# Cached grouped-query attention: K loaded one transfer further ahead, P*V two steps behind, a transposed last P*V, and three V loads with one head group in two half copies

## The chip, the cores and the metric

The kernel runs on one core of one Trainium2 chip. Its engines are TensorE (PE), VectorE (DVE), ScalarE (ACT), GpSimd (POOL) and SyncE (SP), each with a queue of its own, and 16 DMA engines move data between HBM and SBUF. The metric is the device time of one execution in microseconds, as the median of the runs.

## The reference

```python
B, Sq, D = 32, 4, 1024
Hq, Hkv, Sk, Dh = 32, 4, 2048, 128            # everything in bf16

q = (x @ wq).reshape(B, Sq, Hq, Dh).transpose(0, 2, 1, 3)
k = repeat(k_cache, 8, axis=1); v = repeat(v_cache, 8, axis=1)   # caches: [B, 4, 2048, 128]
p = softmax(einsum("bhqd,bhkd->bhqk", q, k) * Dh ** -0.5)
o = einsum("bhqk,bhkd->bhqd", p, v)
return o.transpose(0, 2, 1, 3).reshape(B, Sq, Hq * Dh) @ wo
```

Each of the 32 batch entries has 4 queries of 32 heads. Eight heads share one of the 4 head groups of the caches. The caches are 2 MB of K and 2 MB of V per batch entry, and each byte is used once.

## The kernel before

The loop runs over the batch entries, one per step i. The 4 queries x 8 heads of one head group make 32 rows, and the 4 groups make the 128 rows of the score tile.

Loads. `load_k(b)` (line 132) brings the K of entry b in one transfer of 2048 KB into one of three buffers; it waits until PE has transposed the K that was there (`("fill", b - 3, 7)`). `load_v(b)` (line 137) brings V in the same way into one of three buffers and waits for the P*V that last used it (`("pv", b - 3)`). For the last entry V comes in four transfers, one for each head group. All loads are issued by SP in one queue, in program order; SP stops at the first wait that isn't met. The order is x, four parts of wq, K0, K1, and then for each b: K(b+2), V(b), and for b = 2 to 5 a quarter of wo (lines 152 to 159).

A step i of the loop (lines 320 to 343), in the order in which the engines get it:

1. `pe_qk(i)` (line 235): 16 matmuls give the scores in PSUM (`ps_s`). `softmax_max(i)`: DVE takes the row maximum and scales it.
2. `pe_ot(i-2)`, `ot_evac(i-2)`: the output of entry i-2 is transposed into `oT_sb`. After every eighth entry `oproj` multiplies 32 tokens with wo.
3. `pe_fill(i+1, f)` and `evac(i+1, f)` (lines 201 to 219), f = 0 to 7: PE transposes the next K tile in eight parts, and DVE and ACT copy the parts to `KT_sb`. `softmax_exp(i)` stands after the first two parts on ACT and writes P, not normalised, to `P_sb`; `softmax_rinv(i)` gives one over the row sums.
4. `pe_pv(i-1)` (line 254): 64 matmuls, 16 for each head group, with P^T stationary; `o_evac(i-1)` scales by one over the sum.
5. `pe_pt(i, f)`, `evac_pt(i, f)` (lines 221 to 232): PE transposes P, and DVE copies it to `PT_sb`, once P*V of entry i-1 is done with that buffer.

So P*V runs one step behind its scores, and V(b) follows K(b+2) in the queue. PE's small outputs go through a ring of four PSUM banks (`slot`, line 194), in program order.

After the loop (lines 346 to 378) the last entry is finished by itself: P*V of three head groups, then of the fourth; each result is scaled by ACT, transposed by PE, copied by DVE, and then used by the output projection of the last 32 tokens: 24 heads, then 8. The result is copied to `y_sb`, and the stores go out on SP and ACT.

All waits are semaphore counts, written down by the small planner `_Program` (line 13): each operation names what it waits for, and each engine runs its list in order.

Of the kernel before, what the change touches and what calls it, by code (L numbers as in the profile page):

```python
# [5 lines left out]
ACT = mybir.ActivationFunctionType  # L6
ALU = mybir.AluOpType
AX = mybir.AxisListType
BF16 = mybir.dt.bfloat16
F32 = mybir.dt.float32  # L10


class _Program:
# [43 lines left out]
def bass_standalone__gqa_block_cached__sampling_kernel(  # L57
# [8 lines left out]
    B, Sq, D = x.shape  # L66
    _, G, Sk, Dh = k_cache.shape
# [8 lines left out]
    TV = T // C  # L76
    KT = D // 128
    NKB = 3
    NVB = 3
    NFILL = 8  # L80
    TB = T // NFILL
    NRING = 4
    OG = 8
    NOG = B // OG
    NC = D // 4
    scale = float(Dh) ** -0.5
# [5 lines left out]
    with ExitStack() as es:  # L92
        def sbuf(name, shape, dtype):
            return es.enter_context(nc.sbuf_tensor(name, shape, dtype))
# [4 lines left out]
        V_sb = sbuf("V_sb", [128, NVB, G, TV, Dh], BF16)  # L99
        KT_sb = sbuf("KT_sb", [128, TV, G, R * C], BF16)  # L100
        QT_sb = sbuf("QT_sb", [128, B, Hq, Sq], BF16)
        oT_sb = sbuf("oT_sb", [128, Hq, NT], BF16)
        P_sb = sbuf("P_sb", [128, Sk], BF16)
        PT_sb = sbuf("PT_sb", [128, TV, 128], BF16)
        x_sb = P_sb[:, 0:D]
        xT_sb = P_sb[:, D:2 * D].rearrange("p (a b) -> p a b", b=128)
        o_sb = sbuf("o_sb", [128, Dh], BF16)
# [15 lines left out]
        p = _Program()  # L123
# [8 lines left out]
        def load_k(b):  # L132
            p.dma("sp", lambda e: e.dma_start(
                K_sb[:, b % NKB, :, :], k_cache[b].rearrange("g (r t) d -> (g r) t d", r=R)),
                [("fill", b - NKB, NFILL - 1)] if b >= NKB else [], ("k", b), f"s_k{b % NKB}")

        def load_v(b):
            src = v_cache[b].rearrange("g (p t) d -> p g (t d)", p=128)
            dst = V_sb[:, b % NVB, :, :, :].rearrange("p g t d -> p g (t d)")
            waits = [("pv", b - NVB)] if b >= NVB else []  # L140
            if b < B - 1:
                p.dma("sp", lambda e: e.dma_start(dst, src), waits, ("v", b), f"s_v{b % NVB}")
            else:
                for g in range(G):
                    p.dma("sp", lambda e, g=g: e.dma_start(dst[:, g, :], src[:, g, :]), waits, ("v", b, g), f"s_vl{g}")
# [3 lines left out]
                wo_sb[:, 8 * c:8 * c + 8, :], wo[c * 1024:(c + 1) * 1024, :].rearrange("(h p) n -> p h n", p=128)),  # L149
                ["qproj"], ("wo", c), f"s_w{c}")  # L150

        load_k(0)
        load_k(1)
        for b in range(B):
            if b + 2 < B:
                load_k(b + 2)
            load_v(b)
            if b in (2, 3, 4, 5):
                load_wo(b - 2)
# [34 lines left out]
        def slot(free):  # L194
            n = len(freed)
            freed.append(free)
            return ring[n % NRING], [freed[n - NRING]]
# [13 lines left out]
        def evac(b, f):  # L211
            buf = slot_of["kt", b, f]
            waits = [("fill", b, f)] + ([("qk", b - 1)] if b else [])
            dst = KT_sb[:, f * TB // C:(f + 1) * TB // C, :, :].rearrange("p v g (r c) -> p (v g) r c", c=C)
            src = buf.rearrange("p (c m r) -> p m r c", c=C, r=R)
            if f in DVE_FILLS:
                p.op("dve", lambda e: e.tensor_copy(dst, src), waits, ("kt", b, f))  # L217
            else:
                p.op("act", lambda e: e.activation(dst, src, ACT.Copy), waits, ("kt", b, f))  # L219

        def pe_pt(i, f):
            buf, waits = slot(("pt", i, f))
            buf = slot_of["pt", i, f] = buf.bitcast(BF16)
            for q in range(8):
                p.op("pe", lambda e, q=q: e.transpose(  # L225
                    buf[:, q * 128:(q + 1) * 128], P_sb[:, (8 * f + q) * 128:(8 * f + q + 1) * 128], ident[:, :]),
                    waits + [("exp", i)] if q == 0 else [], ("ptf", i, f) if q == 7 else None)

        def evac_pt(i, f):
            buf = slot_of["pt", i, f]  # L230
            p.op("dve", lambda e: e.tensor_copy(PT_sb[:, 8 * f:8 * f + 8, :].rearrange("p t q -> p (t q)"), buf),  # L231
                 [("ptf", i, f)] + ([("pv", i - 1)] if i else []), ("pt", i, f))


        def pe_qk(i):
# [11 lines left out]
        def pv_mm(buf, i, g, t, waits, done):  # L247
            p.op("pe", lambda e: e.matmul(  # L248
                buf[32 * g:32 * (g + 1), 0:Dh],
                lhsT=PT_sb[:, t, 32 * g:32 * (g + 1)],  # L250
                rhs=V_sb[:, i % NVB, g, t, :],
                start=(t == 0), stop=(t == TV - 1), tile_position=(0, 32 * g)), waits, done)

        def pe_pv(i):
            buf, waits = slot(("o", i))
            slot_of["o", i] = buf
            waits = waits + [("pt", i, 0), ("pt", i, 1), ("v", i)]
            for t in range(TV):
                for g in range(G):
                    pv_mm(buf, i, g, t, waits if t == 0 and g == 0 else [],  # L260
                          ("pv", i) if (t, g) == (TV - 1, G - 1) else None)

        def o_evac(i):
            buf = slot_of["o", i]
            p.op("act", lambda e: e.activation(o_sb[:, :], buf[:, 0:Dh], ACT.Copy, scale=rinv[:, i:i + 1]),  # L265
                 [("pv", i), ("rinv", i)] + ([("oT", i - 1)] if i else []), ("o", i))

        def pe_ot(i):
            buf, waits = slot(("ot", i))
            buf = slot_of["ot", i] = buf.bitcast(BF16)  # L270
            p.op("pe", lambda e: e.transpose(buf[:, 0:128], o_sb[:, :], ident[:, :]), waits + [("o", i)], ("oT", i))  # L271

        def ot_evac(i):
            buf = slot_of["ot", i]
            p.op("act", lambda e: e.activation(  # L275
                oT_sb[:, :, i * Sq:(i + 1) * Sq], buf[:, 0:128].rearrange("p (h s) -> p h s", s=Sq), ACT.Copy),
                [("oT", i)], ("ot", i))
# [38 lines left out]

        for f in range(NFILL):
            pe_fill(0, f)
            evac(0, f)
        for i in range(B):  # L320
            pe_qk(i)
            softmax_max(i)
            if i >= 2:
                pe_ot(i - 2)
                ot_evac(i - 2)
                if i % OG == 1 and i > 1:
                    oproj(i // OG - 1)
            if i + 1 < B:
                for f in (0, 1):
                    pe_fill(i + 1, f)  # L330
                    evac(i + 1, f)
            softmax_exp(i)
            if i + 1 < B:
                for f in range(2, NFILL):
                    pe_fill(i + 1, f)
                    evac(i + 1, f)
            softmax_rinv(i)
            if i >= 1:
                pe_pv(i - 1)
                o_evac(i - 1)  # L340
            for f in range(2):
                pe_pt(i, f)
                evac_pt(i, f)


        L = B - 1
        pe_ot(L - 1)
        ot_evac(L - 1)
        o_l, waits = slot(None)
        waits = waits + [("pt", L, 0), ("pt", L, 1)]  # L350
        for t in range(TV):
            for g in range(3):
                pv_mm(o_l, L, g, t, waits + [("v", L, k) for k in range(3)] if t == 0 and g == 0 else [],
                      ("pva", L) if (t, g) == (TV - 1, 2) else None)
        for t in range(TV):
            pv_mm(o_l, L, 3, t, [("v", L, 3)] if t == 0 else [], ("pv", L) if t == TV - 1 else None)
        p.op("act", lambda e: e.activation(o_sb[0:96, :], o_l[0:96, 0:Dh], ACT.Copy, scale=rinv[0:96, L:L + 1]),
             [("pva", L), ("rinv", L), ("oT", L - 1)], "oa")
        p.op("act", lambda e: e.activation(o_sb[96:128, :], o_l[96:128, 0:Dh], ACT.Copy, scale=rinv[96:128, L:L + 1]),
             [("pv", L)], "ob")  # L360
        ta, waits = slot(None)
        ta = ta.bitcast(BF16)
        p.op("pe", lambda e: e.transpose(ta[:, 0:96], o_sb[0:96, :], ident[0:96, 0:96]), waits + ["oa"], "oTa")
        p.op("dve", lambda e: e.tensor_copy(
            oT_sb[:, 0:24, L * Sq:(L + 1) * Sq], ta[:, 0:96].rearrange("p (h s) -> p h s", s=Sq)), ["oTa"], "ota")
        y_l = ps_s[:, 0:512]
        n = NOG - 1
        oproj_mm(y_l, n, range(24), ["ota", ("ot", L - 1)], None)
        tb, waits = slot(None)
        tb = tb.bitcast(BF16)  # L370
        p.op("pe", lambda e: e.transpose(tb[:, 0:32], o_sb[96:128, :], ident[96:128, 96:128]), waits + ["ob"], "oTb")
        p.op("dve", lambda e: e.tensor_copy(
            oT_sb[:, 24:32, L * Sq:(L + 1) * Sq], tb[:, 0:32].rearrange("p (h s) -> p h s", s=Sq)), ["oTb"], "otb")
        oproj_mm(y_l, n, range(24, 32), ["otb"], ("op", n))
        oproj_evac(y_l, n)
        for m in range(NOG - 1):
            oproj_out(m, ("sp",))
# [57 lines left out]
```

## Time and profile before

| | |
|---|---|
| median of 9 runs | 387.18 us (385.95 to 387.56) |
| profiled execution, its own time | 386.93 us |
| its span, first to last instruction | 385.1 us |
| PE busy | 279.0 us (72%) |
| DVE busy | 273.8 us (71%) |
| ACT busy | 208.6 us (54%) |
| DMA queue of the loads (q1) | 151.49 MB, 96.2% of 16 engines' span |
| K loads | 32 x 2048 KB, 24.9 us from issue to landing |
| V loads | 31 x 2048 KB, 27.0 us; 4 x 512 KB, 15.7 us |

Busy time counts an engine's own instructions, and DMA time is counted in engine time of 16 DMA engines. The time from issue to landing of a load includes its time in the queue behind earlier loads. The mean granted TensorE clock is 0.954 of full speed. A chain of work follows the execution back from its last instruction, from each step to what released it.

### The profile page before, as it was taken

What the parts mean: (1) busy time and instruction counts of PE and PEld (TensorE: products, weight loads), DVE (VectorE), ACT (ScalarE), POOL (GpSimd) and SP (SyncE); (2) the same over time, 40 slices, a digit from 0 to 9 for tenths busy, and PEclk for the clock granted to TensorE, in tenths of its full rate; (3) what the DMA queues carried; (4) which work ended last, traced back from release to release, by engine and by line L of the source; (5) the groups of instructions that cost most, each with busy time, mean ns of one, the idle gap of its engine ahead of it and who ended that gap; (6) DMA issues with size and microseconds to landing.
All of it is one profiled execution on the core that took longest, in us unless ns stands there. A gap on an engine that the chain in (4) does not pass through costs nothing.

```text
span 385.1 us, 12595 instructions
## 1 busy us (share of the span) xinstructions
PE 279.0 (72%) x5929; PEld 227.2 (59%) x5929; DVE 273.8 (71%) x299; ACT 208.6 (54%) x261; POOL 0.7 (0%) x6
## 2 busy tenths in 40 slices
PE   2876888655383967888777778877758878876756
PEld 1875766535272856666655566665647666665545
DVE  0016999783552984899888849998868858997850
ACT  1005777455161646676666627766646557666620
POOL 0000000000000000000000000000000000000000
PEclk9998999996977899999999999999998999999978
DMA  8999999999999999999999999999999999999930
GB/s 327 434 425 419 416 419 397 413 412 395 411 403 416 417 419 413 418 413 419 416 416 421 415 416 416 416 411 418 415 418 419 418 415 421 413 421 411 380 149 9
DMA packets 27251, 152.32 MB, mean 395 GB/s; under 512 B 1472, under 2 KB 1984, under 8 KB 22592
## 3 DMA queue, kind: packets, MB, share of 16 engines
q1 hardware_dynamic: 27104, 151.49, 96.2%
q8 instruction: 46, 0.75, 0.8%
q10 hardware_dynamic: 96, 0.03, 0.0%
q14 instruction: 5, 0.04, 0.0%
HBM read 151.26 MB, written 0.26 MB: 393 GB/s over the span
## 4 chain that ended last, share of the span: by engine, by line
DMA 58%; PE 17%; ACT 12%; DVE 10%; issue 2%; SPq 0%
DMA K_sb<-in_k_cache_dram 52%; ACT KT_sb L219 6%; DMA w_sb<-in_wq_dram 6%; ACT P_sb L285 6%; DVE KT_sb L217 5%; DVE mx L280 4%; PE ps_r L207 3%; PE ps_r L248 3%; PE ps_r L296 3%; PE ps_s L240 3%; PE ps_r L225 3%; PE ps_s L296 1%; PE ps_s L176 1%; DVE QT_sb L187 0%; DVE PT_sb L231 0%
## 5 line engine op out<-in xcount | busy, mean ns | idle before, releaser
L207 PE MATMUL ps_r<-ident,K_sb 128*128 128x128 bf16 x2048 | 140.7, 227 | 66.6 <-DMA K_sb<-in_k_cache_dram 39.3
L217 DVE COPY KT_sb<-ps_r 128x1024 bf16<-128x1024 bf16 x128 | 147.9, 1215 | 38.8 <-PE ps_r L207 38.7
L207 PEld LDWEIGHTS ps_r<-ident,K_sb 128*128 128x128 bf16 x2048 | 123.5, 102 | 82.9 <-DMA K_sb<-in_k_cache_dram 41.5
L219 ACT ACTIVATE KT_sb<-ps_r 128x1024 bf16<-128x1024 bf16 x128 | 124.5, 1026 | 72.1 <-PE ps_r L207 71.9
L280 DVE TENSOR_REDUCE mx<-ps_s 128x1 f32<-128x2048 f32 x32 | 73.3, 2291 | 7.6 <-PE ps_s L240 7.3
L285 ACT ACTIVATE P_sb<-ps_s,negmx 128x2048 bf16<-128x2048 f32 x32 | 63.0, 1970 | 2.1 <-DVE negmx L281 2.1
L231 DVE COPY PT_sb<-ps_r 128x1024 bf16<-128x1024 bf16 x64 | 41.4, 686 | 16.6 <-PE ps_r L225 15.0
L248 PE MATMUL ps_r<-V_sb,PT_sb 128*32 128x128 bf16 x2048 | 36.7, 222 | 17.1 <-ACT KT_sb L219 12.3
L248 PEld LDWEIGHTS ps_r<-V_sb,PT_sb 128*32 128x32 bf16 x2048 | 31.0, 98 | 22.7 <-ACT KT_sb L219 19.4
L275 ACT ACTIVATE oT_sb<-ps_r 128x128 bf16<-128x128 bf16 x31 | 8.6, 278 | 55.6 <-PE ps_r L271 55.6
L225 PE MATMUL ps_r<-ident,P_sb 128*128 128x128 bf16 x512 | 35.1, 223 | 2.0 <-ACT P_sb L285 1.4
L240 PE MATMUL ps_s<-KT_sb,QT_sb 128*32 128x512 bf16 x512 | 34.7, 389 | 2.3 <-DVE KT_sb L217 1.7
L225 PEld LDWEIGHTS ps_r<-ident,P_sb 128*128 128x128 bf16 x512 | 29.4, 99 | 5.6 <-ACT P_sb L285 1.6
L240 PEld LDWEIGHTS ps_s<-KT_sb,QT_sb 128*32 128x32 bf16 x512 | 10.9, 96 | 13.3 <-issue 3.3
L187 DVE CAST QT_sb<-ps_r 128x512 bf16<-128x512 f32 x2 | 1.3, 686 | 22.4 <-PE ps_r L176 22.4
L265 ACT ACTIVATE o_sb<-ps_r,rinv 128x128 bf16<-128x128 f32 x31 | 11.4, 367 | 9.6 <-PE ps_r L248 9.6
L189 ACT ACTIVATE QT_sb<-ps_r 128x512 bf16<-128x512 f32 x2 | 1.1, 594 | 25.9 <-PE ps_r L176 25.9
L176 PE MATMUL ps_s<-P_sb,w_sb 128*128 128x128 bf16 x128 | 9.3, 230 | 7.4 <-DMA w_sb<-in_wq_dram 7.4
L296 PE MATMUL ps_r<-w_sb,oT_sb 128*32 128x256 bf16 x384 | 11.5, 273 | 3.5 <-issue 2.3
L176 PEld LDWEIGHTS ps_s<-P_sb,w_sb 128*128 128x128 bf16 x128 | 8.1, 103 | 8.0 <-issue 4.3
L296 PEld LDWEIGHTS ps_r<-w_sb,oT_sb 128*32 128x32 bf16 x384 | 10.0, 97 | 4.6 <-issue 3.4
L271 PEld LDWEIGHTS ps_r<-ident,o_sb 128*128 128x128 bf16 x31 | 3.0, 98 | 12.7 <-issue 12.7
(30 smaller groups left out, 58.7 us busy)
## 6 DMA issues: line engine op xcount, KB each, us to landing
K_sb<-in_k_cache_dram SPq DMA_DIRECT2D x32, 2048.0 KB, 24.9
V_sb<-in_v_cache_dram SPq DMA_DIRECT2D x31, 2048.0 KB, 27.0
w_sb<-in_wq_dram SPq DMA_DIRECT2D x4, 2048.0 KB, 14.8
w_sb<-in_wo_dram SPq DMA_DIRECT2D x4, 2048.0 KB, 24.6
V_sb<-in_v_cache_dram SPq DMA_DIRECT2D x4, 512.0 KB, 15.7
P_sb<-in_x_dram SPq DMA_DIRECT2D x1, 256.0 KB, 2.8
out_dram<-y_sb SPq DMA_DIRECT2D x14, 16.0 KB, 11.6
out_dram<-y_sb ACTq DMA_DIRECT2D x2, 16.0 KB, 1.6
```

Source lines behind the costliest of these rows:

```text
L176: p.op("pe", lambda e, kt=kt, h=h: e.matmul(ps_q(h), lhsT=w_sb[:, kt, h * Dh:(h + 1) * Dh], rhs=xT_sb[:, kt, :], start=(kt == 0 and h % 4 ...
L207: p.op("pe", lambda e, q=q, t=t: e.transpose(buf[:, q * 128:(q + 1) * 128], K_sb[:, b % NKB, t, :], ident[:, :]), waits + [("k", b), "iden ...
L217: p.op("dve", lambda e: e.tensor_copy(dst, src), waits, ("kt", b, f))
L219: p.op("act", lambda e: e.activation(dst, src, ACT.Copy), waits, ("kt", b, f))
L225: p.op("pe", lambda e, q=q: e.transpose(buf[:, q * 128:(q + 1) * 128], P_sb[:, (8 * f + q) * 128:(8 * f + q + 1) * 128], ident[:, :]), wai ...
L231: p.op("dve", lambda e: e.tensor_copy(PT_sb[:, 8 * f:8 * f + 8, :].rearrange("p t q -> p (t q)"), buf), [("ptf", i, f)] + ([("pv", i - 1)] ...
L240: p.op("pe", lambda e, c=c, g=g: e.matmul(ps_s[32 * g:32 * (g + 1), c * 512:(c + 1) * 512], lhsT=QT_sb[:, i, REP * g:REP * (g + 1), :], rh ...
L248: p.op("pe", lambda e: e.matmul(buf[32 * g:32 * (g + 1), 0:Dh], lhsT=PT_sb[:, t, 32 * g:32 * (g + 1)], rhs=V_sb[:, i % NVB, g, t, :], star ...
L265: p.op("act", lambda e: e.activation(o_sb[:, :], buf[:, 0:Dh], ACT.Copy, scale=rinv[:, i:i + 1]), [("pv", i), ("rinv", i)] + ([("oT", i - ...
L280: p.op("dve", lambda e: e.tensor_reduce(mx[:, i:i + 1], ps_s[:, :], AX.X, ALU.max), [("qk", i)], ("mx", i))
L285: p.op("act", lambda e: e.activation(P_sb[:, :], ps_s[:, :], ACT.Exp, bias=negmx[:, i:i + 1], scale=scale, accum_out=ssum[:, i:i + 1]), [( ...
L296: p.op("pe", lambda e, h=h, j=j: e.matmul(buf[32 * j:32 * (j + 1), 0:NC], lhsT=oT_sb[:, h, 32 * n:32 * (n + 1)], rhs=wo_sb[:, h, NC * j:NC ...
```

## The change

Four things change.

- The loads: K0, K1 and K2 are issued first, and then K(b+3) before V(b). So each K goes out one transfer earlier in the queue than before.
- P*V of an entry runs two steps behind its scores (`pe_pv(i - 2)`), and its output is transposed three steps behind. For that `PT_sb` has two buffers, and the copy of P^T waits for the P*V of two entries before.
- The last entry: P is multiplied by one over its sums on DVE before it is transposed. Its P*V then has V as the stationary operand, so that it gives the transposed output o^T of one head group straight away; four such groups alternate with the four parts of the last output projection. The scaling on ACT and the transposes of the output are gone for this entry.
- V of entries 7, 15 and 23: head groups 0 to 2 come in one transfer, and group 3 in two copies for 64 partitions each. The DRAM side of these copies has 8 rows as its outer dimension.

```diff
+def _load_low_half(nc, eng, dst, src):
+    assert src.shape[0] == 8 and eng.engine == mybir.EngineType.SP
+    return eng.add_instruction(mybir.InstDMACopy(
+        name=nc.get_next_instruction_name(),
+        engine=eng.engine,
+        mode="Copy",
+        queue="qSPDynamicHW",
+        cce_op=ALU.bypass,
+        ins=[eng.lower_ap_dma(src)[0]],
+        outs=[eng.lower_ap_dma(dst)[0]],
+    ))
...
+    LOW_V = (7, 15, 23)
...
-        PT_sb = sbuf("PT_sb", [128, TV, 128], BF16)
+        PT_sb = sbuf("PT_sb", [128, 2, TV, 128], BF16)
...
-            if b < B - 1:
+            if b in LOW_V:
+                p.dma("sp", lambda e: e.dma_start(dst[:, 0:3, :], src[:, 0:3, :]), waits, ("v", b, 0), f"s_v{b % NVB}")
+                low = v_cache[b, 3].rearrange("(j a t) d -> j a (t d)", j=2, a=8)
+                for j in range(2):
+                    p.dma("sp", lambda e, j=j: _load_low_half(nc, e, dst[64 * j:64 * (j + 1), 3, :], low[j]),
+                          waits, ("v", b, 1) if j == 0 else ("v", b), "s_vlow")
+            elif b < B - 1:
...
-        load_k(0)
-        load_k(1)
+        for b in range(NKB):
+            load_k(b)
         for b in range(B):
-            if b + 2 < B:
-                load_k(b + 2)
+            if b + NKB < B:
+                load_k(b + NKB)
             load_v(b)
...
-                 [("ptf", i, f)] + ([("pv", i - 1)] if i else []), ("pt", i, f))
+                 [("ptf", i, f)] + ([("pv", i - 2)] if i > 1 else []), ("pt", i, f))
...
-            if i >= 2:
-                pe_ot(i - 2)
-                ot_evac(i - 2)
-                if i % OG == 1 and i > 1:
+            if i >= 3:
+                pe_ot(i - 3)
+                ot_evac(i - 3)
+                if i > OG and i % OG == 2:
                     oproj(i // OG - 1)
...
-            if i >= 1:
-                pe_pv(i - 1)
-                o_evac(i - 1)
+            if i >= 2:
+                pe_pv(i - 2)
+                o_evac(i - 2)
+            if i == L:
+                p.op("dve", lambda e: e.tensor_scalar(P_sb[:, :], P_sb[:, :], rinv[:, L:L + 1], None, op0=ALU.mult),
+                     [("rinv", L)], ("pn", L))
             for f in range(2):
-                pe_pt(i, f)
+                pe_pt(i, f, ("pn", L) if i == L else ("exp", i))
                 evac_pt(i, f)
...
+        pe_ot(L - 2)
+        ot_evac(L - 2)
+        pe_pv(L - 1)
+        o_evac(L - 1)
...
+        def pv_last(g):
+            buf, waits = slot(None)
+            for t in range(TV):
+                p.op("pe", lambda e, t=t: e.matmul(
+                    buf[:, 0:32], lhsT=V_sb[:, L % NVB, g, t, :], rhs=PT_sb[:, L % 2, t, 32 * g:32 * (g + 1)],
+                    start=(t == 0), stop=(t == TV - 1)),
+                    waits + [("v", L, g), ("pt", L, 0), ("pt", L, 1)] if t == 0 else [],
+                    ("pvl", g) if t == TV - 1 else None)
+            p.op("dve", lambda e: e.tensor_copy(
+                oT_sb[:, 8 * g:8 * (g + 1), L * Sq:(L + 1) * Sq], buf[:, 0:32].rearrange("p (h s) -> p h s", s=Sq)),
+                [("pvl", g)], ("otl", g))
+
+        def oproj_last(g):
+            oproj_mm(y_l, n, range(8 * g, 8 * (g + 1)), [("otl", g), ("ot", L - 1), ("exp", L)],
+                     ("op", n) if g == G - 1 else None)
+
+        pe_ot(L - 1)
+        ot_evac(L - 1)
+        pv_last(0)
+        for g in range(G):
+            if g + 1 < G:
+                pv_last(g + 1)
+            oproj_last(g)
```

The old code for the last entry (lines 349 to 374 of the kernel before) is taken out.

More of the change, by code (lines that the diff above doesn't have):

```diff
@@ L219, in evac, with pe_pt @@
                 p.op("act", lambda e: e.activation(dst, src, ACT.Copy), waits, ("kt", b, f))
-        def pe_pt(i, f):
+        def pe_pt(i, f, ready):
             buf, waits = slot(("pt", i, f))
@@ L226, in pe_pt @@
                     buf[:, q * 128:(q + 1) * 128], P_sb[:, (8 * f + q) * 128:(8 * f + q + 1) * 128], ident[:, :]),
-                    waits + [("exp", i)] if q == 0 else [], ("ptf", i, f) if q == 7 else None)
+                    waits + [ready] if q == 0 else [], ("ptf", i, f) if q == 7 else None)
         def evac_pt(i, f):
             buf = slot_of["pt", i, f]
-            p.op("dve", lambda e: e.tensor_copy(PT_sb[:, 8 * f:8 * f + 8, :].rearrange("p t q -> p (t q)"), buf),
-                 [("ptf", i, f)] + ([("pv", i - 1)] if i else []), ("pt", i, f))
+            p.op("dve", lambda e: e.tensor_copy(PT_sb[:, i % 2, 8 * f:8 * f + 8, :].rearrange("p t q -> p (t q)"), buf),
+                 [("ptf", i, f)] + ([("pv", i - 2)] if i > 1 else []), ("pt", i, f))
         def pe_qk(i):
@@ L249, in pv_mm @@
                 buf[32 * g:32 * (g + 1), 0:Dh],
-                lhsT=PT_sb[:, t, 32 * g:32 * (g + 1)],
+                lhsT=PT_sb[:, i % 2, t, 32 * g:32 * (g + 1)],
                 rhs=V_sb[:, i % NVB, g, t, :],
@@ L256, in pe_pv @@
             slot_of["o", i] = buf
-            waits = waits + [("pt", i, 0), ("pt", i, 1), ("v", i)]
+            waits = waits + [("pt", i, 0), ("pt", i, 1), ("v", i)] + ([("v", i, 0)] if i in LOW_V else [])
             for t in range(TV):
@@ L319, in bass_standalone__gqa_block_cached__sampling_kernel @@
             evac(0, f)
+        L = B - 1
         for i in range(B):
@@ L322, in bass_standalone__gqa_block_cached__sampling_kernel @@
             softmax_max(i)
-            if i >= 2:
-                pe_ot(i - 2)
-                ot_evac(i - 2)
-                if i % OG == 1 and i > 1:
+            if i >= 3:
+                pe_ot(i - 3)
+                ot_evac(i - 3)
+                if i > OG and i % OG == 2:
                     oproj(i // OG - 1)
-            if i + 1 < B:
+            if i < L:
                 for f in (0, 1):
@@ L332, in bass_standalone__gqa_block_cached__sampling_kernel @@
             softmax_exp(i)
-            if i + 1 < B:
+            if i < L:
                 for f in range(2, NFILL):
@@ L343, in bass_standalone__gqa_block_cached__sampling_kernel @@
                 evac_pt(i, f)
-        L = B - 1
+        pe_ot(L - 2)
+        ot_evac(L - 2)
+        pe_pv(L - 1)
+        o_evac(L - 1)
+        y_l = ps_s[:, 0:512]
+        n = NOG - 1
+        def pv_last(g):
[9 more added lines that the diff above has]
+                [("pvl", g)], ("otl", g))
@@ L347, in bass_standalone__gqa_block_cached__sampling_kernel @@
+        def oproj_last(g):
+            oproj_mm(y_l, n, range(8 * g, 8 * (g + 1)), [("otl", g), ("ot", L - 1), ("exp", L)],
+                     ("op", n) if g == G - 1 else None)
         pe_ot(L - 1)
         ot_evac(L - 1)
[L349 to L371, printed above, removed]
@@ L372, in bass_standalone__gqa_block_cached__sampling_kernel @@
-        p.op("dve", lambda e: e.tensor_copy(
-            oT_sb[:, 24:32, L * Sq:(L + 1) * Sq], tb[:, 0:32].rearrange("p (h s) -> p h s", s=Sq)), ["oTb"], "otb")
-        oproj_mm(y_l, n, range(24, 32), ["otb"], ("op", n))
+        pv_last(0)
[3 more added lines that the diff above has]
+            oproj_last(g)
         oproj_evac(y_l, n)
```

## The prediction

> **What bounds the kernel now.** I read the slices of the page, then the DMA queues, then the last 36 us in stretches, then the chain of work that ended last. From the page:
>
> ```profile
> PEclk9998999996977899999999999999998999999978
> DMA  8999999999999999999999999999999999999930
> GB/s 327 434 425 419 416 419 397 413 412 395 411 403 416 417 419 413 418 413 419 416 416 421 415 416 416 416 411 418 415 418 419 418 415 421 413 421 411 380 149 9
> q1 hardware_dynamic: 27104, 151.49, 96.2%
> q8 instruction: 46, 0.75, 0.8%
> HBM read 151.26 MB, written 0.26 MB: 393 GB/s over the span
> ```
>
> The DMA engines are full from the second slice to the 37th, near 416 GB/s. PE is busy for 72%, DVE for 71%; neither is the bound. A 2048 KB load (2.097 MB) costs 2.097 / 416 = 5.04 us. The bytes stay, so only what happens after the last bytes, or how these end, can be gained. Now the end in stretches; the last two columns are DMA share and GB/s:
>
> ```profile
> core 0: us, PE busy (x) PEld busy (x) DVE busy (x) ACT busy (x) POOL busy (x), PEclk, DMA share, GB/s
> 362.00:364.00 2.00, 0.82 (x15) 0.49 (x16) 2.00 (x3) 2.00 (x4) 0.00 (x0) 1.00 1.03 404
> 364.00:366.00 2.00, 2.00 (x84) 1.79 (x88) 1.06 (x3) 1.18 (x2) 0.00 (x0) 1.00 0.74 280
> 366.00:368.00 2.00, 1.17 (x18) 0.39 (x17) 1.85 (x3) 0.28 (x1) 0.00 (x0) 1.00 0.58 224
> 368.00:370.00 2.00, 1.02 (x61) 0.88 (x64) 1.51 (x2) 0.42 (x1) 0.00 (x0) 1.00 0.50 199
> 370.00:372.00 2.00, 0.58 (x15) 0.41 (x16) 0.16 (x1) 1.89 (x3) 0.00 (x0) 0.60 0.50 191
> 372.00:374.00 2.00, 1.69 (x16) 1.42 (x14) 1.07 (x2) 0.28 (x1) 0.00 (x0) 0.50 0.29 92
> ```
>
> Half of the 16 engines run dry near 365; the other half works alone, at half the rate, until 373.7 (the last V load is issued at 357.96 and lands 15.7 us later). The shares from 364 on add up to (0.74 + 0.58 + 0.50 + 0.50 + 0.29) x 2 = 5.2 us of all 16 engines: dealt out evenly, the loads would end near 369.3. One group of 8 is some 8 us behind the other. Then the chain, start and length in us:
>
> ```profile
> 333.92 24.47 DMA K_sb<-in_k_cache_dram
> 358.44 0.63 PE ps_r L207 x8
> ...
> 369.58 2.07 ACT P_sb L285 x2
> 371.64 0.05 issue
> 371.69 1.90 PE ps_r L225 x16
> ...
> 374.36 3.08 PE ps_r L248 x61
> ...
> 377.89 2.81 PE ps_s L296 x96
> ```
>
> The end hangs on the last K tile, which lands on its slowest engine at 358.40. From there to the end of the span is 26.7 us: transposing K, scores, softmax, P^T, P*V, output projection. V lands just before P^T is ready, so it does not decide. PEclk is 0.50 in this stretch: 64 P*V matmuls take 3.08 us, where they take 1.08 us at full clock (358 to 366).
>
> [...]46 packets of 0.75 MB in all on q8. They take 0.8% x 16 x 385 = 49 us of engine time; dealt to 8 engines that is 6.2 us each, near the 8 us lag. That is my reading of the lag, not shown. [...]PEclk is 0.5 from 370.4 to 377.2[...].
>
> **The change, part by part.**
>
> *K one transfer earlier.* The order of the tail goes from K30 V28 K31 V29 V30 V31 to K31 V28 V29 V30 V31. K31 lands one load earlier: -5.04 us. The price is less cover elsewhere. At the start V0 no longer lies between K2 and K3. K3 waits for the transposes of K0 and is issued at 34.2; K2 (issued at 4.03, 35.3 us to landing) ends at 39.3 on the slowest engine and a little before 38 on the others, so K3 still queues some 2 us before the rings run dry: nothing, at worst 1 to 2 us. Later, V(b) waits for a P*V two steps behind: its issue comes about 10 - 5 = 5 us later against its slot. Around V28 to V30 a load waits 25 to 28 us from issue to landing, some 20 us of that in the queue, so 5 us less is hidden. V31 was the tightest, 15.7 us to landing, and stays behind V29 and V30 in the queue, 10 us of transfers.
>
> *P^T in two buffers, P*V a step later.* Same instructions, same order within a step; the copy of P^T then waits for the P*V of two steps ago, issued just ahead of it, as now. Nothing. But for the last two steps it moves work: P*V of step 30 now stands behind the last P^T instead of ahead of it.
>
> *Three loads with low halves.* Per load, 512 KB goes to 8 engines instead of 16. Each of the 8 gets 32 KB more, the other 8 get 32 KB less; 32 KB at 26 GB/s (416 / 16) is 1.26 us. Three loads: 3.8 us either way, which is half of the 8 us lag. If the low half is the early one, K31 and V31 land 3.8 us earlier on the late engines, and the two halves end together near 369.9 (373.7 - 3.8). SP gets 6 more DMA issues of about 1.2 us (L145's own are 0.3 to 1.3), in a queue that waits 10 us a step: nothing.
>
> *The tail.* K31 lands at 358.40 - 5.04 - 3.8 = 349.6. Up to the end of the last exp the work is the same and takes 371.64 - 358.40 = 13.2 us, since V28 and V29 land within it (354.6, 359.7): 362.8. Then
> - reciprocal and its wait 0.2: 363.0.
> - new: P times 1/sum, 128x2048 in bf16. The trace has no such row[...]. 363.7.
> - P^T 1.9 at half clock[...]: 365.7. The transpose of step 29, 0.2: 365.9.
> - P*V of step 30, 3.1 at half clock; V30 landed at 364.7. 369.0. Its copy and its transpose, with waits, 0.7: 369.7.
> - removed: the old last P*V, two copies, two transposes and their copies.
> - new: 4 groups of 16 matmuls with V stationary, 128 columns, and 32 moving. The nearest rows are the transposes (L176, 16 in 0.89 us at full clock: 56 ns); the moving side is a quarter. [...]I take 45: 0.7 a group, 2.8 in all.
> - output projection 4 x 32 matmuls at 29 ns (L296, 96 in 2.81): 3.7. The copies on DVE (about 0.2) lie under the next group. V31 lands at 369.9 and its last group is wanted near 373.5: not on the path.
> - 376.2; pipeline end, copy of y 0.7; then the last stores, which took 385.1 - 382.6 = 2.5: 379.4.
>
> The span falls from 385.1 to 379.4. The profiled execution's own time was 386.93, 1.8 over its span, and the median of the runs is 0.25 above that: 379.4 + 1.8 + 0.25 = 381.4. In sum: -5.0 (K slot), -3.8 (balance), +3.1 (a longer tail: 29.8 us from K31 instead of 26.7).
>
> **The rivals.**
> 1. *The low half is the late half.* The trace does not number the engines. Then K31 lands 3.8 later instead of earlier, at 357.2, and the sum gives 381.4 + 7.6 = 389.0: slower. It decides once the shift makes the late engines more than 2 us later. For it: nothing but that half and half are alike in the page. Against it: the size, 3.8 us on each side, is just half of the lag.
> 2. *The copies run on all engines, or the lag is not tied to fixed engines.* Only the slot and the tail are left: 381.4 + 3.8 = 385.2, a small gain.
> 3. *PE bounds the end.* The final matmuls find PE still at half clock, where a transpose took 119 ns (1.90 / 16) instead of 56[...]: 384.5 to 386.3.
> 4. The other way: PE stays at full clock after the idle stretch. Then P^T and P*V take 1.0 and 1.1 and the end is 2.9 earlier, 378.5.
>
> **How the numbers follow.** The forecast with rival 4 as its good end: 0.70, its own range 378.4 to 384.5. Rival 1: 0.12. Rival 2: 0.08. Rival 3: 0.10. The predicted time is 381.4. The range leaves out rival 1 and the better edge: 378.4 to 386.6. About 0.2% (0.8 us) can be told from no change. Faster: 0.70, nearly all of rival 2 and most of rival 3, 0.84. Same: 0.04. Slower: 0.12, rival 1.
>
> **What would show it.** In the changed kernel's profile the DMA share should stay near 1.0 until 367 or later and drop to zero within 3 us, with no stretch at 0.5; if the stretch at 0.5 grows to some 15 us, rival 1 is right; if it keeps its 8 us, rival 2. The last K tile should land near 349.6 and the last exp end near 362.8. The matmuls of the new last P*V should take about 0.7 us a group; over 1.2 us, with PEclk at 0.5, is rival 3. A share under 0.9 between 35 and 60 us would mean that the shorter cover at the start cost time.

## The result

The changed kernel takes 397.92 us (median of 10 runs, 395.46 to 399.14) against 387.18 us before. The ratio is 1.027, with a 95% interval of 1.026 to 1.029: 10.7 us slower. The prediction was 381.4 us and faster. Its profiled execution took 398.35 us, with a span of 396.6 us against 385.1.

From the page of the changed kernel, the slices of the span and the queue of the loads:

```profile
DMA  8999999999999999999999999999999999999860
GB/s 342 421 426 420 416 418 397 407 401 411 410 396 413 416 258 417 418 416 415 418 414 416 333 334 414 417 418 414 418 415 418 321 357 415 401 415 403 328 249 26
...
q1 hardware_dynamic: 26816, 151.49, 96.6%
```

The bytes are the same as before, and the DMA engines are as busy. But three times they are busy and move much less: 258 GB/s near 144 us, 333 and 334 near 228 us, 321 and 357 near 317 us (the middle of the slices). These are the places of entries 7, 15 and 23, the three loads with half copies. Against 416 GB/s the five slices of 9.9 us lack 158 + 83 + 82 + 95 + 59 = 477 GB/s, or 4.7 MB: 11.4 us at the full rate. That alone is larger than the slowdown.

The packets of the changed kernel by size:

```profile
DMA packets 26963, 152.32 MB, mean 384 GB/s; under 512 B 1520, under 2 KB 2032, under 8 KB 22256
```

and of the kernel before:

```profile
DMA packets 27251, 152.32 MB, mean 395 GB/s; under 512 B 1472, under 2 KB 1984, under 8 KB 22592
```

The 92 DMAs of before leave 16 packets under 512 B each (92 x 16 = 1472), one for each engine by my reading. The six half copies add 48, 8 each: they run on 8 engines. The prediction had assumed this, and its "low half" is these 8 engines; the trace does not number them.

The first of the three closer up, in stretches of the changed kernel (the last two columns are DMA share and GB/s):

```profile
134.00:138.00 4.00, 3.17 (x99) 2.19 (x92) 3.72 (x6) 1.36 (x3) 0.00 (x0) 1.00 1.09 429
138.00:142.00 4.00, 3.51 (x59) 3.17 (x59) 3.95 (x5) 3.44 (x3) 0.00 (x0) 1.00 1.00 224
142.00:146.00 4.00, 0.49 (x8) 0.31 (x6) 2.14 (x3) 2.28 (x4) 0.00 (x0) 0.81 1.04 273
146.00:150.00 4.00, 1.12 (x44) 1.16 (x48) 0.00 (x0) 0.00 (x0) 0.00 (x0) 0.50 0.89 312
150.00:154.00 4.00, 4.00 (x63) 2.58 (x52) 1.38 (x2) 0.37 (x1) 0.00 (x0) 0.50 1.02 411
```

A DMA share of 1.0 at half the GB/s means that each packet takes twice its time on average: in the trace a packet of 16 KB takes 1.21 us in the mean from 138 to 142 us, against 0.62 from 100 to 130, and one of 4 KB 0.28 against 0.16. PE then stands idle (busy for 0.49 us of 4) because V has not landed. In the chain of waits the half copies (L17, the new helper's line) show up where there was no V before:

```profile
112.06 5.72 PE ps_r L229 x56
117.79 0.38 SPq L158
118.16 0.04 issue
118.21 5.99 SPq L17
124.20 0.05 issue
124.25 24.54 DMA V_sb<-in_v_cache_dram
```

And the end, in stretches:

```profile
374.00:378.00 4.00, 3.63 (x98) 2.23 (x97) 3.21 (x6) 1.46 (x4) 0.00 (x0) 1.00 0.61 210
378.00:382.00 4.00, 1.85 (x64) 1.63 (x64) 2.22 (x2) 1.92 (x2) 0.00 (x0) 0.75 1.04 413
382.00:384.00 2.00, 0.67 (x11) 0.62 (x8) 0.92 (x2) 0.60 (x3) 0.00 (x0) 0.50 0.45 132
384.00:386.00 2.00, 2.00 (x41) 1.80 (x43) 1.38 (x2) 0.28 (x1) 0.00 (x0) 0.50 0.13 53
...
388.00:390.00 2.00, 2.00 (x75) 1.74 (x72) 0.38 (x2) 0.18 (x1) 0.00 (x0) 1.00 0.13 48
```

The stretch at half share is gone, as forecast for a balance that works. But in its place stands a stretch of some 7 us at a share of 0.13: two of 16 engines are still at work. The dip ahead of it (0.61) is the wait for a buffer for the last V, which is issued only at 375.3, when P*V of entry 28 is done with that buffer.

The chain does not hang on these last bytes, though. The last load that it names lands at 315.3, and all that follows is work of PE, ACT and DVE:

```profile
286.55 28.80 DMA K_sb<-in_k_cache_dram
...
322.19 1.83 issue
324.01 1.08 PE ps_r L270 x64
...
365.51 1.08 PE ps_r L270 x64
...
374.16 1.08 PE ps_r L270 x64
```

The "issue" that ends at 324.01 is a wait that the profile does not name. By its time it is the wait for V of entry 23: the last of the landings that the trace records for its half copies is at 323.92. From there on one step of the loop follows the other (8.65 us apart at the end), and no load decides, if only just: K of entry 31 landed at 368.5 on its slowest engine, not at 349.6 as forecast, and PE came to it 0.2 us later.

### The profile page after: what moved, and what is told of

It is laid out like the page before. It is cut to its first block, busy times and chain, and to the rows that moved or that the text cites. A ratio compares the mean times of both kernels' runs of the same rounds, so it can differ in the third digit from the quotient of the medians.

```text
span 396.6 us, 12597 instructions
## 1 busy us (share of the span) xinstructions
PE 283.9 (72%) x5927; PEld 230.2 (58%) x5927; DVE 274.9 (69%) x302; ACT 207.7 (52%) x259; POOL 0.7 (0%) x6
## 4 chain that ended last, share of the span: by engine, by line
DMA 51%; PE 20%; ACT 14%; DVE 9%; issue 3%; SPq 2%
DMA K_sb<-in_k_cache_dram 45%; ACT KT_sb L241 7%; DMA V_sb<-in_v_cache_dram 6%; ACT P_sb L307 6%; PE ps_r L229 5%; DVE KT_sb L239 5%; PE ps_r L247 4%; PE ps_s L262 4%; PE ps_r L270 3%; DVE mx L302 3%; PE ps_r L318 3%; SPq L17 2%; PE ps_s L318 1%; DVE PT_sb L253 1%; PE ps_r L382 0%
## 5 line engine op out<-in xcount | busy, mean ns | idle before, releaser
L270 PE MATMUL ps_r<-V_sb,PT_sb 128*32 128x128 bf16 x1984 | 35.8, 228 | 26.0 <-ACT KT_sb L241 8.9
L270 PEld LDWEIGHTS ps_r<-V_sb,PT_sb 128*32 128x32 bf16 x1984 | 30.2, 101 | 31.1 <-ACT KT_sb L241 14.5
L262 PE MATMUL ps_s<-KT_sb,QT_sb 128*32 128x512 bf16 x512 | 36.7, 403 | 3.8 <-DVE KT_sb L239 1.7
L247 PE MATMUL ps_r<-ident,P_sb 128*128 128x128 bf16 x512 | 37.3, 230 | 1.7 <-DVE P_sb L365 1.3
L247 PEld LDWEIGHTS ps_r<-ident,P_sb 128*128 128x128 bf16 x512 | 31.3, 103 | 5.6 <-DVE P_sb L365 1.6
L287 ACT ACTIVATE o_sb<-ps_r,rinv 128x128 bf16<-128x128 f32 x31 | 11.4, 367 | 22.7 <-PE ps_r L270 22.7
```

The lines of the kernel that those rows point to most:

```text
L247: p.op("pe", lambda e, q=q: e.transpose(buf[:, q * 128:(q + 1) * 128], P_sb[:, (8 * f + q) * 128:(8 * f + q + 1) * 128], ident[:, :]), wai ...
L262: p.op("pe", lambda e, c=c, g=g: e.matmul(ps_s[32 * g:32 * (g + 1), c * 512:(c + 1) * 512], lhsT=QT_sb[:, i, REP * g:REP * (g + 1), :], rh ...
L270: p.op("pe", lambda e: e.matmul(buf[32 * g:32 * (g + 1), 0:Dh], lhsT=PT_sb[:, i % 2, t, 32 * g:32 * (g + 1)], rhs=V_sb[:, i % NVB, g, t, : ...
```

## The experiments

Theory A said that the half copies slow all traffic; theory B that the new order of the loads and of P*V takes their cover away.

**Whole loads in the changed kernel.**

```diff
-    LOW_V = (7, 15, 23)
+    LOW_V = ()
```

> The changed kernel with every V load whole again (no half copies); all else as changed. Theory A (the half copies themselves slow all DMA traffic: three stretches near 250 to 330 GB/s in the changed kernel, 3 to 4 us each): these stretches vanish, DMA stays near 416 GB/s, the half of the engines is again some 8 us late, and the time is 385 us, a little under before (ratio 0.993 to 0.998). Theory B (K a slot earlier and P*V a step later take the cover of the loads away): the time stays above 392 us and the low stretches stay.

Measured: 382.91 us, ratio to before 0.992 (0.989 to 0.995). The low stretches are gone:

```profile
GB/s 330 432 426 425 415 413 416 411 393 410 406 407 409 420 420 418 415 408 416 421 415 414 417 420 412 420 412 418 416 415 418 418 414 416 417 424 408 352 317 32
```

The half copies cost the whole loss: the two ratios differ by 0.035, or 13.6 us. Theory B falls. The rest of the change is a gain of 3 us (ratio 0.992).

**Only the half copies, in the kernel before.** The three loads cut as in the change, nothing else.

> The kernel before with only the three V loads of entries 7, 15 and 23 cut into 1536 KB and two half copies. Theory A: three stretches of low GB/s, 10 to 13 us slower than before (397 to 400 us). Theory B: no slower than before, 384 to 388 us.

Measured: 400.84 us, ratio 1.039 (1.036 to 1.041), 14.4 us slower than the runs of before beside it. Theory A holds in both kernels.

**Half copies with rows of 4 KB on all engines.**

```diff
-                low = v_cache[b, 3].rearrange("(j a t) d -> j a (t d)", j=2, a=8)
                 for j in range(2):
-                    p.dma("sp", lambda e, j=j: _load_low_half(nc, e, dst[64 * j:64 * (j + 1), 3, :], low[j]),
+                    p.dma("sp", lambda e, j=j: e.dma_start(dst[64 * j:64 * (j + 1), 3, :], src[64 * j:64 * (j + 1), 3, :]),
```

> The changed kernel, but the two half copies have 64 rows of 4 KB on the DRAM side instead of 8 rows of 32 KB: same bytes, same halves of the partitions, packets of 4 KB on all 16 engines. Theory A1 (the 32 KB packets slow the others): no low stretches, 384 to 386 us. Theory A2 (many engines writing into one half of the partitions get in each other's way): a loss stays, some 0.6 us per copy, 3 to 4 us in all, 388 to 390 us.

Measured: 393.17 us, ratio 1.019 (1.016 to 1.021). The 32 KB packets are gone, and 10.3 us of the loss stay. From 130 to 160 us the loads move 11.07 MB, and 115 packets are under 512 B. At 16 for each 2.097 MB the bytes account for some 84 of them, which leaves some 15 more for each of the two copies: by this estimate they run on all 16 engines. So neither packets of 32 KB nor copies on 8 engines are needed for the loss. The size was missed: I had expected 3 to 4 us.

**Four quarter copies with rows of 16 KB, 8 engines.**

```diff
-                low = v_cache[b, 3].rearrange("(j a t) d -> j a (t d)", j=2, a=8)
-                for j in range(2):
-                    p.dma("sp", lambda e, j=j: _load_low_half(nc, e, dst[64 * j:64 * (j + 1), 3, :], low[j]),
+                low = v_cache[b, 3].rearrange("(j a t) d -> j a (t d)", j=4, a=8)
+                for j in range(4):
+                    p.dma("sp", lambda e, j=j: _load_low_half(nc, e, dst[32 * j:32 * (j + 1), 3, :], low[j]),
```

> The changed kernel, but head group 3 of the three loads comes in four copies of 32 partitions with 8 rows of 16 KB each: still 8 engines, but packets of 16 KB as in the K loads, and two copies write each half of the partitions. Theory A1: hardly any low stretch, and the balance works: 380 to 383 us. Theory A2: low stretches of about half the depth, 386 to 393 us.

Measured: 394.06 us, ratio 1.022 (1.017 to 1.026). Again 11 us over whole loads, a little past the range for theory A2. The same count gives some 8 packets under 512 B for each copy (121 of them from 130 to 160 us, 11.52 MB): 8 engines. Packets of 16 KB are what K comes in all the time (2048 KB in 128 packets), so the packet size is out as the whole cause.

**One copy of all partitions.** Head group 3 of the three loads in one copy of 128 partitions.

> The changed kernel, but head group 3 of the three loads comes in one copy of all 128 partitions. If cutting a load in two costs nothing and only copies to half of the partitions cost, the time is that of the version with whole loads, 382 to 384 us, with no low stretches. If the cutting itself costs, 390 us or more.

Measured: 382.98 us, ratio 0.991 (0.989 to 0.992), as with whole loads. Cutting a load in two costs nothing; cutting it across the partitions did.

What is special about half of the partitions? Theory P says that engines which write into the same partitions hold each other up, theory H that any copy of 64 partitions is slow. The trace does not number the engines, so no run here shows which engine writes which partitions. That a copy of partitions 0 to 63 would bring engines together, and one of 32 to 95 would not, was my assumption. The next two runs test it by their times: they differ only in the partitions, and in the rows of DRAM that go into them.

```diff
-                p.dma("sp", lambda e: e.dma_start(dst[:, 0:3, :], src[:, 0:3, :]), waits, ("v", b, 0), f"s_v{b % NVB}")
+                p.dma("sp", lambda e: e.dma_start(dst[:, 0:2, :], src[:, 0:2, :]), waits, ("v", b, 0), f"s_v{b % NVB}")
+                for g in (2, 3):
+                    p.dma("sp", lambda e, g=g: e.dma_start(dst[32:96, g, :], src[32:96, g, :]),
+                          waits, ("v", b, 1) if g == 2 else ("v", b), "s_vlow")
```

**Partitions 32 to 95.**

> The changed kernel, but of the three loads head groups 2 and 3 come in one copy each, of partitions 32 to 95 alone (rows of 4 KB, all 16 engines); partitions 0 to 31 and 96 to 127 of these two groups are left out, 1.5 MB in all, worth 3.8 us at 416 GB/s. Theory P ([...]two engines that write into one set hold each other up): [...]no low stretches and some 379 us. Theory H (any copy of 64 partitions is slow): low stretches, 386 us or more.

Measured: 379.20 us, ratio 0.981 (0.980 to 0.983).

**Partitions 0 to 63** (`0:64` in place of `32:96`).

> As the run with partitions 32 to 95, but partitions 0 to 63 are loaded, and 64 to 127 of these two groups are left out: same bytes, packets and engines. Theory P: [...]the low stretches are back, 7 to 10 us more than with partitions 32 to 95 (386 to 390 us). Theory H: the same time as with 32 to 95.

Measured: 390.60 us, ratio 1.011 (1.007 to 1.014). The same bytes in copies of the same form: 11.4 us apart. The stretches around the first of the three loads, first of the run with 32 to 95:

```profile
138.00:142.00 4.00, 3.51 (x61) 3.17 (x59) 3.95 (x5) 3.67 (x3) 0.00 (x0) 1.00 1.05 439
142.00:146.00 4.00, 3.07 (x101) 2.21 (x98) 3.06 (x5) 2.41 (x5) 0.00 (x0) 1.00 0.96 393
```

and of the run with 0 to 63:

```profile
138.00:142.00 4.00, 3.48 (x56) 3.13 (x56) 3.93 (x4) 3.11 (x3) 0.00 (x0) 1.00 1.08 236
142.00:146.00 4.00, 0.62 (x8) 0.45 (x8) 2.47 (x4) 2.60 (x4) 0.00 (x0) 1.00 0.97 285
```

From 138 to 142 us the share is full in both (1.05 and 1.08); the rate is 439 GB/s with partitions 32 to 95 and 236 with 0 to 63.

**Partitions 0 to 63, in copies of 8 rows.**

```diff
+                for n in range(4):
+                    g, j = 2 + n // 2, n % 2
+                    low = v_cache[b, g].rearrange("(j a t) d -> j a (t d)", j=4, a=8)
+                    p.dma("sp", lambda e, g=g, j=j, low=low: _load_low_half(nc, e, dst[32 * j:32 * (j + 1), g, :], low[j]),
+                          waits, ("v", b, 1 + n) if n < 3 else ("v", b), "s_vlow")
```

> As the run with partitions 0 to 63 (64 to 127 of the two groups left out), but by 8 engines: four copies of 32 partitions with 8 rows of 16 KB on the DRAM side[...]. Theory P: no low stretches. The 8 engines move what they move in a whole load, the other 8 are 7.5 us ahead in sum: if these others are the late half, the two halves end together and the time falls to 375 to 378 us; if the 8 engines are the late half, their lag grows to 15 us and the time stays at 382 to 384 us. Theory H: low stretches, 386 us or more.

Measured: 381.06 us, ratio 0.986 (0.984 to 0.987), and no low stretch (its slices hold 413 GB/s or more from the 13th to the 33rd). So the lower half as such is harmless, and so are copies on 8 engines. The quarter copies above had the same form (32 partitions, 8 rows of 16 KB) and lost 11 us; half of them went to partitions 64 to 127. So neither the form of a copy nor its partitions alone decide, but both together. Theory P with my assumption is not contradicted by these runs, but it is not shown by them. They do not separate writing from reading either: with other partitions an engine may also read other rows of DRAM.

The time lies between the two that I had named for the late half, and its end says why:

```profile
363.00:366.00 3.00, 0.00 (x0) 0.00 (x0) 0.92 (x2) 2.24 (x3) 0.00 (x0) 1.00 0.93 344
366.00:368.00 2.00, 1.98 (x31) 1.78 (x35) 0.99 (x2) 0.19 (x1) 0.00 (x0) 0.58 0.25 86
368.00:370.00 2.00, 1.60 (x60) 1.33 (x52) 0.40 (x1) 0.43 (x2) 0.00 (x0) 0.56 0.17 61
370.00:372.00 2.00, 1.84 (x65) 1.74 (x65) 0.38 (x2) 0.30 (x2) 0.00 (x0) 1.00 0.12 48
```

Fourteen engines end together near 366, two are some 6 us late (a share of 0.12 is two of 16). With whole loads eight are late (a share of 0.56 and 0.55 from 368 to 372 us). The 8 engines spared here are therefore six of the late eight and two of the early ones. The late engines are not the upper half, nor the lower: two of them are among the 8 that such copies use. The packets of the changed kernel say the same. Only the half copies, on their 8 engines, move packets of 32 KB, 48 in all. In the third of the three loads twelve of these 16 packets start between 307.9 and 312.6 us, and the other four, two engines' worth, between 316.9 and 320.8.

**One load with half copies instead of three** (`LOW_V = (15,)`).

> The changed kernel with the half copies in one load (entry 15) instead of three. If each load with half copies costs the same, 4 to 5 us (the three cost some 13.5 us against whole loads), the time is 386.5 to 388 us, with one low stretch in the GB/s. If the cost comes from the three together, 383 to 384 us.

Measured: 387.50 us, ratio 1.002 (1.001 to 1.003), with one low stretch (345 and 306 GB/s). That is 4.6 us over whole loads by the times, 3.9 by the ratios to the runs of before beside each. A third of the 13.6 us above is 4.5: the cost goes about with the number of such loads.

**The new end alone, in the kernel before.**

> The kernel before with only the new end: P of the last entry normalised, its P*V by head group with V stationary, no change of the loads or of the other steps. If the gain of the version with whole loads (3.5 us) comes from K landing one transfer earlier, this end alone gains 0 to 1.5 us (385 to 386.5). If it comes from the end itself, 382 to 384 us.

Measured: 387.40 us, ratio 1.002 (1.001 to 1.003). The new end by itself gains nothing, a bit less than the 0 to 1.5 us expected. The gain of the version with whole loads needs K one transfer earlier, with P*V two steps behind; what each of these two would do alone was not tried.

**What makes eight engines late.** In the version with whole loads:

```diff
+            twice = f in (2, 3, 4, 5)
...
-                    waits + [("k", b), "ident"] if q == 0 else [], ("fill", b, f) if q == TB - 1 else None)
+                    waits + [("k", b), "ident"] if q == 0 else [], None if twice or q < TB - 1 else ("fill", b, f))
+                if twice:
+                    p.op("pe", lambda e, q=q, t=t: e.transpose(
+                        buf[:, q * 128:(q + 1) * 128], K_sb[:, b % NKB, t, :], ident[:, :]),
+                        [], ("fill", b, f) if q == TB - 1 else None)
```

> The version with whole loads, with 32 transposes of each K tile done twice: 2048 more PE instructions, so 8 more packets of 16 KB on the instruction queue q8 (54 instead of 46), PE time of at most 1.8 us a step, mostly in gaps. If the lag of 8 DMA engines comes from fetching PE's instructions, it grows from 8 us by a sixth, 1.3 us: the last V part lands 1.3 us later and the time rises by 0.5 to 2 us. If the lag has another cause, the stretch at half DMA share keeps its length.

Measured: 387.97 us, ratio 1.004 (1.002 to 1.005). The instruction queue, and the issue and landing of the same load (K of entry 28), here:

```profile
q8 instruction: 54, 0.88, 0.9%
...
298.99 0.72 SPq L149 DMA_DIRECT2D K_sb<-in_k_cache_dram  x1
K_sb<-in_k_cache_dram SPq DMA_DIRECT2D x1, 2048.0 KB, 24.3
```

and with whole loads alone:

```profile
q8 instruction: 46, 0.75, 0.8%
...
296.44 2.91 SPq L149 DMA_DIRECT2D K_sb<-in_k_cache_dram  x1
K_sb<-in_k_cache_dram SPq DMA_DIRECT2D x1, 2048.0 KB, 25.3
```

The load lands on its slowest engine at 299.0 + 24.3 = 323.3 against 296.4 + 25.3 = 321.7: 1.6 us later, as expected of fetches that fall on 8 engines (1.3 us). The first engine to land it is not later (313.6 against 313.9 us), though the load is issued 2.5 us later: the queue was still full. By then 42 of the 54 packets had started, against 36 of the 46. The time rose by 5 us where 0.5 to 2 were expected: PE was 94% busy from 250 to 300 us (47.1 of 50), and most likely became a bound of its own. So the time is no measure of the lag.

The trace of the kernel before shows the lag grow, fetch by fetch. It has 16 landings for each load, one for each engine by my reading, though it does not say which engine it is:

| a load that its first engine lands at | fetches started by then | the other engines behind the first |
|---|---|---|
| 13.1 us | 0 | all within 0.5 us |
| 18.0 us | 1 | one by 1.9, the rest within 0.5 |
| 32.6 us | 2 | two by 1.7, the rest within 0.5 |
| 68.0 us | 6 | six by 1.7 to 2.0, the rest within 0.5 |
| 353.9 us | 42 | eight by 7.6 to 9.6, the rest within 2.4 |

Each fetch sets one engine back by some 1.2 to 1.4 us, more than the 1.07 us that its packet takes, and the fetches come round to eight engines.

**A PE without its last wait**, again with whole loads:

```diff
             if i == L:
+                warm, waits = slot("warm")
+                warm = warm.bitcast(BF16)
+                for q in range(48):
+                    p.op("pe", lambda e, q=q: e.transpose(
+                        warm[:, (q % 8) * 128:(q % 8 + 1) * 128], K_sb[:, L % NKB, q, :], ident[:, :]),
+                        waits if q == 0 else [], "warm" if q == 47 else None)
```

> The version with whole loads, with 48 idle transposes on PE (their result is used by nothing) between P*V of step 29 and the last P^T, where PE waits for the last softmax some 3 us. If the half clock in the end is paid for on the path, P^T (1.65 us) and P*V of step 30 (1.9 us) take 1.0 and 1.1 and the time falls by 1 to 1.5 us, to 381.4 to 382. If another wait takes over (V of step 30 lands at 368.4), it falls by less than 0.5 us.

Measured: 382.52 us, ratio 0.989 (0.987 to 0.991), not to be told apart from 382.91. The two steps did get faster, here:

```profile
367.34 1.07 PE L247 MATMUL ps_r<-ident,P_sb 128*128 128x128 bf16 x16
...
368.63 1.08 PE L270 MATMUL ps_r<-V_sb,PT_sb 128*32 128x128 bf16 x64 [0.16 <-DMA V_sb<-in_v_cache_dram]
```

against, with whole loads alone:

```profile
367.59 1.65 PE L247 MATMUL ps_r<-ident,P_sb 128*128 128x128 bf16 x16 [3.06 <-DVE P_sb L365]
...
369.28 1.90 PE L270 MATMUL ps_r<-V_sb,PT_sb 128*32 128x128 bf16 x64
```

The 1.4 us won are lost again further on. Part of it is a wait for V (0.16 us above). The larger part is the clock: the half clock was not avoided, it came later. From 372 to 378 us, here:

```profile
372.00:374.00 2.00, 1.44 (x33) 0.75 (x22) 0.00 (x0) 0.00 (x0) 0.00 (x0) 0.72 0.27 90
374.00:376.00 2.00, 2.00 (x46) 1.34 (x42) 0.19 (x1) 0.00 (x0) 0.00 (x0) 0.50 0.00 0
```

and with whole loads alone:

```profile
372.00:374.00 2.00, 2.00 (x74) 1.75 (x72) 0.38 (x2) 0.27 (x1) 0.00 (x0) 1.00 0.22 71
374.00:376.00 2.00, 1.76 (x55) 1.22 (x51) 0.19 (x1) 0.00 (x0) 0.00 (x0) 1.00 0.00 0
```

So this run does not show what an end at full clock would be worth. Its profiled execution was also the slowest of its four (383.64 us). The version with whole loads, the one with group 3 in one copy and this one are the fastest here that compute everything.

## Why the prediction was wrong

**The step that failed** is the one on the three loads: "Each of the 8 gets 32 KB more, the other 8 get 32 KB less; 32 KB at 26 GB/s (416 / 16) is 1.26 us. Three loads: 3.8 us either way". It priced a DMA engine by the bytes that it moves. It did not ask which partitions the copies write. The runs showed that this counts: the same bytes in copies of the same form cost 11.4 us more in partitions 0 to 63 than in 32 to 95. Around the first of the half copies all traffic goes at 224 to 312 GB/s for some 12 us. The price was some 4 to 4.6 us for each load, 13.6 in all, in place of a gain of 3.8. None of the rivals had it.

A smaller term was off too: SP's issues of the six half copies, taken at about 1.2 us, took 0.6 to 7.8. The run with twelve copies by 8 engines in place of the six has no low stretch, so the number of issues is not what costs.

**The balance** was wrong in a second way. Two of the late engines are among the 8 that got the extra bytes, on top of their lag; this is rival 1 for 2 of 8 engines. A load counts as landed with its slowest engine, and in the changed kernel these two were last: for the third load with half copies they made the P*V of entry 23 wait until 324.0, and they brought K31 in at 368.5. By the same estimate of 1.26 us a load that is 3.8 us later for the last engine where I had 3.8 earlier; it was not measured apart from the conflict.

**The lag's cause** was read rightly: PE's instruction fetches, on 8 engines. Its size was taken a little low: 6.2 us by the time of the packets, where the landings show 7.6 to 9.6.

**K one transfer earlier and the tail** held. Without the half copies the sum is that of rival 2, and it had K31 at 358.40 - 5.04 = 353.4. The chain of the version with whole loads:

```profile
331.53 21.78 DMA K_sb<-in_k_cache_dram
...
364.49 2.07 ACT P_sb L307 x2
...
366.78 0.77 DVE P_sb L365
...
367.59 1.65 PE ps_r L247 x16
...
369.35 1.86 PE ps_r L270 x34
...
371.96 0.86 PE ps_r L382 x32
372.82 0.99 PE ps_s L318 x32
```

K31 landed at 353.3; the last exp ended at 366.6 (353.4 + 13.2 = 366.6). The multiplication took 0.77 us; the 0.7 that the sum has for it rested on no run. P^T took 1.65 (1.9 in the sum), P*V of step 30 1.9 (3.1), a group of the new P*V 0.43 to 0.50 (0.7). The span was 381.2, where the sum without balance gives 379.4 + 3.8 = 383.2: P*V of step 30, 1.2 us shorter, and the cheaper groups make up the 2 us. That P*V was not quicker by the clock, which was at 0.50 from 367.9 to 371.3. The length of this stretch, 3.4 us here, was an assumption in the range of rival 3. The 3.1 us had been read from the last P*V of before, which runs in two passes, three head groups and then the fourth; with all four together it is 1.9 at half clock. The normalising and the new matmuls were not the risk.

**The cover of the loads** held too: with whole loads, no slice at the start is under 393 GB/s after the first. What I had not seen is that V31 waits for the P*V of entry 28. In the changed kernel that stands in the chain of compute steps behind 324.0, so V31 is issued only at 375.3, and engines that are done with V30 stand idle (share 0.61 from 374 to 378).

## What to carry to other kernels

For a DMA engine count the bytes that it moves, and ask which partitions each copy writes. Here copies of partitions 0 to 63 slowed everything in flight beside them at a full DMA share (236 GB/s at 1.08), and copies of the same form in 32 to 95 did not (439 GB/s at 1.05). So read share and GB/s together: a full share at half the rate says that packets take longer (1.21 us in place of 0.62 for 16 KB), not that there is too little work.

To even out DMA engines, find out first which of them are late. The share at the end tells how many, not which; the landings of each load tell when the lag arose.

## What was not expected of the hardware

- Six copies of 256 KB, worth some 0.6 us each by their bytes at 416 GB/s, made the kernel 11.4 us slower in partitions 0 to 63 than in 32 to 95 (390.60 against 379.20 us), 1.9 us a copy. Why this is three times the 0.6 us is open.
- Fetching PE's instructions, 46 packets of 16 KB, sets 8 of the 16 DMA engines back by 7.6 to 9.6 us over some 355 us. Two of these 8 engines are among the 8 that the half copies use.
- The last P*V with V stationary, 16 matmuls with 128 columns stationary and 32 moving, took 0.43 to 0.50 us a group at full clock, 27 to 31 ns each.
